# Attention probabilities: transposed on TensorE, or in two of six query tiles by a DRAM round trip and VectorE's 32x32 blocks

## The chip, the cores and the metric

One core of one Trainium2 chip runs the whole kernel as one program. The metric is the device time of one execution in microseconds. The kernel before takes 623.03 us (median of three runs, 622.12 to 624.79).

## The reference

Hash-masked attention over 4 batches of 8 heads, 768 positions and 64 channels, and behind it a gated block on the joined heads:

```python
mask = q_bucket[:, :, :, None] == k_bucket[:, :, None, :]
scores = np.where(mask, scale * np.matmul(q, k.transpose(0, 1, 3, 2)), -1000000000.0)
attn = np.exp(scores - np.max(scores, axis=-1, keepdims=True))
attn = attn / (np.sum(attn, axis=-1, keepdims=True) + 1e-09)
x = np.matmul(attn, v)                      # heads joined to 512 channels
gate = 1.0 / (1.0 + np.exp(-gate_pre))      # gate_pre: causal convolution of x, 5 taps
out = gate * (x @ w_val) @ w_out
```

A bucket is 6 sign bits of a projection. All of it is float32.

## The kernel before

There are 32 **heads** `u` (batch by head) and 6 query **tiles** of 128 rows in each; the main loop runs over the 192 tiles, and **step** `k` is one pass of it. Tile `k` is tile `t = k % 6` of head `k // 6`. Its stages are spread over several steps:

- Scores (line 266, TensorE) are issued one step ahead, in step `k - 1`: 128 x 768 of them, into one of two PSUM buffers `s`. The buffer comes free when the exponentials of tile `k - 2` have read it.
- In step `k` VectorE takes the row maximum `nm` (line 272) and makes factor and shift (`gs` line 278, `nb` line 282); ScalarE computes the exponentials into `p` (line 290), which has four buffers.
- In step `k + 2` GpSimd normalises `p` (line 305).
- In step `k + 3` TensorE transposes `p` in six 128 x 128 blocks (line 314) into two PSUM tiles `tp`, at the end of the step; at the start of step `k + 4` ScalarE copies them to `pt` (line 323), ahead of the exponentials of that step.
- When the sixth tile of a head is copied, `attn_v` (line 337) begins: two of its six rounds of four matmuls `av` in each odd step. ScalarE copies the result to `x` (line 345).

Beside this run side jobs, a few instructions in each step: the preparation of the head after next (`prep`: casts on GpSimd at lines 170 and 173, then six DMAs between partitions at lines 174 to 182, the next raw load at line 148, and for every second head a load of values `vt`, line 154), the convolution (`pair_x`, VectorE, line 368, with a rounding cast `xh` at line 357) and the matrix products of the gated block (`moe`, TensorE, lines 399 and 424, with a rounding cast `hh` at line 408). In some heads' steps the block has no work; in most it issues four matmuls a step.

The orders on TensorE, VectorE, ScalarE and GpSimd are the order of the code. SyncE's queue of DMAs is set by the scheduler that builds the program, and each DMA's wait stands in that queue: what is behind it waits too.

Of the kernel before, what the change touches and what calls it, by code (L numbers as in the profile page):

```python
# [26 lines left out]
def kernel(  # L27
# [13 lines left out]
    D = 64  # L41
# [2 lines left out]
    NP = H // 2  # L44
    KW = 5
    LAG = 3
    scale = 1.0 / float(D) ** 0.5
    NB = 6
    M = D + 2 * NB
# [4 lines left out]
    vp = ctx.enter_context(tc.tile_pool(name="vp", bufs=2))  # L54
    pp = ctx.enter_context(tc.tile_pool(name="pp", bufs=LAG + 1))
    small = ctx.enter_context(tc.tile_pool(name="small", bufs=6))
    ptp = ctx.enter_context(tc.tile_pool(name="ptp", bufs=6))
    xp = ctx.enter_context(tc.tile_pool(name="xp", bufs=2))
    xs = ctx.enter_context(tc.tile_pool(name="xs", bufs=10))
    gp = ctx.enter_context(tc.tile_pool(name="gp", bufs=5))  # L60
# [83 lines left out]
    def load_raw(i):  # L144
        if i < len(units):
            b, h = units[i]
            raws[i] = raw.tile([P, S], FP32, name="r")
            nc.sync.dma_start(out=raws[i], in_=qk[b, h])

    def load_values(i):  # L150
        b, h = units[i]
# [132 lines left out]
    def exponentials(k):  # L284
        s, nb = ss.pop(k), nbs.pop(k)
        p = pp.tile([P, 2, HS], FP32, name="p")
        if k % 2 == 0:
            cur["sm"] = small.tile([P, 2, 2], FP32, name="sm")
        sm = cur["sm"]
        nc.scalar.activation(out=p, in_=s[:, :, 0:HS], func=AF.Exp, bias=nb, scale=gs.pop(k), accum_out=sm[:, k % 2, 0:1])  # L290
        ps[k] = (p.rearrange("p a b -> p (a b)"), sm)


# [9 lines left out]
    def normalise(k):  # L303
        p, _ = ps[k]
        nc.gpsimd.tensor_scalar(out=p, in0=p, scalar1=rcs.pop(k), scalar2=1.0, op0=ALU.mult, op1=ALU.mult)  # L305

    def transposes(k):
        p, _ = ps.pop(k)
        tps[k] = []
        for a in range(2):  # L310
            tp = ps_t.tile([P, 512], FP32, name="tp")
            for n in range(3):
                kb = 3 * a + n
                nc.tensor.transpose(out=tp[:, n * P:(n + 1) * P], in_=p[:, kb * P:(kb + 1) * P], identity=ident)  # L314
            tps[k].append(tp)

    def keep_transposed(k):
        i, qt = tiles[k]
        if qt % 3 == 0:
            cur["pts"].append([ptp.tile([P, 3, HS], FP32, name="pt") for _ in range(2)])  # L320
        qo = (qt % 3) * P
        for pt, tp in zip(cur["pts"][-1], tps.pop(k)):
            nc.scalar.copy(out=pt[:, :, qo:qo + P], in_=tp[:, 0:HS].rearrange("p (a b) -> p a b", b=P))  # L323
        if qt == KB - 1:
            avs.append(attn_v(i, cur["pts"]))
            cur["pts"] = []

    def attn_v(i, pts):
        b, h = units[i]
        hh, c = h % 2, h // 2  # L330
        av = ps_v.tile([P, 512], FP32, name="av")
        vt = vts[i]
        for kb in range(KB):
            if kb:
                yield
            for s, pt in enumerate(pts):
                nc.tensor.matmul(out=av[s * D:(s + 1) * D, 0:HS], lhsT=vt[:, kb, hh * D:(hh + 1) * D], rhs=pt[kb // 3][:, kb % 3, :],  # L337
                                 start=(kb == 0), stop=(kb == KB - 1), tile_position=(0, s * D))
        if hh == 0:
            x = cur["x"] = xp.tile([P, S + KW - 1], FP32, name="x")  # L340
            nc.gpsimd.memset(x[:, 0:KW - 1], 0.0)
        x = cur["x"]
        for s in range(2):
            o = KW - 1 + s * HS
            nc.scalar.copy(out=x[hh * D:(hh + 1) * D, o:o + HS], in_=av[s * D:(s + 1) * D, 0:HS])  # L345
        if hh == 1:
            if c == 0:
                cur["xs"], cur["g"] = {}, []
            convs.append(pair_x(b, c, x, cur["g"], cur["xs"]))

    def pair_x(b, c, x, gs, xs_):
        for o in (0, HS):
            xh = xs.tile([P, HS], FP32R, name="xh")
            xl = xs.tile([P, HS], FP32R, name="xl")
            xs_[(c, o)] = (xh, xl)
            x0 = x[:, KW - 1 + o:KW - 1 + o + HS]
            nc.vector.tensor_copy(out=xh, in_=x0)  # L357
            nc.gpsimd.tensor_tensor(out=xl, in0=x0, in1=xh.bitcast(FP32), op=ALU.subtract)  # L358
        yield
        g = gp.tile([P, S], FP32, name="g")  # L360
        gs.append(g)
        for k in range(KW):
            yield
            w = cw_sb[:, c * KW + k:c * KW + k + 1]
            if k == 0:
                nc.gpsimd.tensor_scalar(out=g, in0=x[:, 0:S], scalar1=w, scalar2=1.0, op0=ALU.mult, op1=ALU.mult)  # L366
            else:
                nc.vector.scalar_tensor_tensor(out=g, in0=x[:, k:k + S], scalar=w, in1=g, op0=ALU.mult, op1=ALU.add)  # L368
        if c == NP - 1:
            yield  # L370
            for g in gs:
                nc.scalar.activation(out=g, in_=g, func=AF.Sigmoid)
            cur["gates"] = 2
            moes.append(moe(b, xs_, gs))
# [9 lines left out]
    def moe(b, xs_, g):  # L384
        hs = {}
        todo = []

        def later():
            while todo:
                todo.pop(0)()  # L390

        def val(o, j):
            acc = acc_tile()
            m = 0
            for wi, xi in ((0, 0), (1, 0), (0, 1)):
                if m:
                    yield
                for c in range(NP):
                    nc.tensor.matmul(out=acc[:, 0:HS], lhsT=wv[wi][:, c, j * P:(j + 1) * P],  # L399
                                     rhs=xs_[(c, o)][xi], start=(m == 0), stop=(m == 11))  # L400
                    m += 1
                later()
            ht = hp.tile([P, HS], FP32, name="ht", bufs=2)
            nc.vector.tensor_tensor(out=ht, in0=acc[:, 0:HS], in1=g[j][:, o:o + HS], op=ALU.mult)  # L404

            def split():
                hh = hp.tile([P, HS], FP32R, name="hh")
                nc.vector.tensor_copy(out=hh, in_=ht)  # L408
                hl = hp.tile([P, HS], FP32R, name="hl")
                nc.gpsimd.tensor_tensor(out=hl, in0=ht, in1=hh.bitcast(FP32), op=ALU.subtract)  # L410
                hs[(o, j)] = (hh, hl)
            todo.append(split)
            yield

        def outp(o, tb):
            for gens in weights:
                finish(gens)
            acc = acc_tile()
            m = 0
            for hi, wi in ((0, 0), (0, 1), (1, 0)):  # L420
                if m:
                    yield
                for j in range(NP):
                    nc.tensor.matmul(out=acc, lhsT=hs[(o, j)][hi][:, tb * P:(tb + 1) * P],  # L424
                                     rhs=wo[wi][:, j, :], start=(m == 0), stop=(m == 11))
                    m += 1
                later()
            ob = op.tile([P, 512], FP32, name="o")
            if cur["gates"]:
                nc.vector.tensor_copy(out=ob, in_=acc)  # L430
            else:
                nc.scalar.copy(out=ob, in_=acc)
            r0 = o + tb * P
            nc.sync.dma_start(out=out[b, r0:r0 + P, :], in_=ob)
            yield

        def idle(n):
            for _ in range(n):
                later()
                yield  # L440

        def hold():
            while len(moes) < 2 and not cur["end"]:
                yield

        chunks = [(val, 0, j) for j in range(NP)]
        chunks += [(val, HS, 0)] + [(outp, 0, tb) for tb in range(3)] + [(val, HS, j) for j in range(1, NP)]
        chunks += [(idle, 2)] + [(outp, HS, tb) for tb in range(3)]
        if b < B - 1:
            chunks.insert(-2, (hold,))  # L450
        for f, *args in chunks:
            yield from f(*args)
# [3 lines left out]
    tiles = [(i, qt) for i in range(len(units)) for qt in range(KB)]  # L456

    raws, stacks, vts, ss, nbs, ps, tps, sums, rcs, nms, gs, cur = {}, {}, {}, {}, {}, {}, {}, {}, {}, {}, {}, {}
    avs, convs, moes, early = [], [], [], {}
    accs = [(ps_m, "m")]  # L460

# [9 lines left out]
        while gens:  # L471
            step(gens)

    cur["gates"], cur["end"], cur["pts"] = 0, False, []
    N = len(tiles)
    with tc.manual_schedule(engines=ENGINES):
        for i in range(5):
# [10 lines left out]
        ahead = [early_bits()]  # L488
        turn = 0
        for k in range(N + LAG + 1):  # L490
            if 0 <= k - LAG - 1:
                keep_transposed(k - LAG - 1)
            pair = k % 2 == 0 and 0 <= k - 2 < N
            if k < N:
# [6 lines left out]
                recip(k - 2)  # L501
            if 0 <= k - 2 < N:
                normalise(k - 2)
            if k < N:
                shifts(k)
            if k + 1 < N:
# [3 lines left out]
                scores(k + 1)  # L510
            if k < N:
                exponentials(k)
            if k >= 60 or k % 2:
                step(convs)
            for _ in range((1, 0, 2, 0, 2, 2)[k % 6]):
# [10 lines left out]
            if k % 2:  # L526
                step(avs)
                step(avs)
            if 0 <= k - LAG < N:
                transposes(k - LAG)  # L530
        accs[:] = [(ps_m, "m"), (ps_t, "tp"), (ps_s, "s"), (ps_t, "tp"), (ps_s, "s")]
        finish(avs)
# [65 lines left out]
```

## Time and profile before

| | us |
|---|---|
| median of three runs | 623.03 |
| span of the profiled execution, first to last instruction | 620.8 |
| busy in it: TensorE matmul / VectorE / ScalarE / GpSimd | 585.5 / 437.6 / 421.4 / 395.6 |
| the steps that the change touches, by ScalarE's exponentials | 175.4 to 545 |
| mean busy share of the 16 DMA engines in those steps | 0.34 |

The profile gives the profiled execution no time but its span; the 2.2 us between the span and the median of the runs lie around the program. Span times count from the first instruction. In a row of groups stand the line, the engine, the operation, what it writes and reads, the count, then the busy time, the mean of one in ns, and the engine's idle time ahead with what ended it. PE is TensorE, DVE VectorE, ACT ScalarE, POOL GpSimd, SPq the queue of SyncE.

### The profile page before, as it was taken

The numbers are of one execution on the slowest core, as the hardware profiler recorded it, in microseconds if no ns is written. First come the engines' busy times: TensorE is split into PE (matmuls) and PEld (weight loads), VectorE is DVE, ScalarE is ACT, GpSimd is POOL, SyncE is SP. The second block draws the span as 40 slices with busy tenths as digits, with TensorE's granted clock in tenths as the row PEclk, the third lists the DMA queues.
The fourth block names the chain that finished last, engine by engine and source line by source line (L and its number), as shares of the span: only waits on it lengthen the run. The fifth ranks groups of instructions, "written<-read, shape, count | busy, mean of one in ns | idle before, by whom it ended". The sixth has DMA issues, their size and how long they took to land.

```text
span 620.8 us, 10648 instructions
## 1 busy us (share of the span) xinstructions
PE 585.5 (94%) x3496; PEld 423.4 (68%) x3496; DVE 437.6 (70%) x1017; ACT 421.4 (68%) x881; POOL 395.6 (64%) x373
## 2 busy tenths in 40 slices
PE   5789898989999999999999999999999999999997
PEld 2655565555657777776767777777667877775895
DVE  5869798998975866668575867569665877665532
ACT  2777777778778666777787676777787766765400
POOL 3576868778766765578564777568764777544321
PEclk9799999999999999999999999999999999999999
DMA  6467666564532235243433234333422213200111
GB/s 227 123 197 199 200 167 208 157 175 118 133 83 68 70 79 142 72 108 82 122 82 107 61 80 126 84 115 82 108 70 78 67 42 91 69 18 1 51 52 51
DMA packets 29031, 64.64 MB, mean 104 GB/s; under 512 B 4937, under 2 KB 10057, under 8 KB 28977
## 3 DMA queue, kind: packets, MB, share of 16 engines
q1 hardware_dynamic: 28832, 63.93, 37.8%
q8 instruction: 28, 0.46, 0.3%
q14 instruction: 27, 0.21, 0.1%
q10 hardware_dynamic: 144, 0.03, 0.0%
HBM read 30.60 MB, written 7.86 MB: 62 GB/s over the span
## 4 chain that ended last, share of the span: by engine, by line
PE 66%; DVE 12%; ACT 12%; DMA 5%; issue 3%; POOL 2%; SPq 1%; ACTq 0%; POOLq 0%; DVEq 0%
PE av L337 17%; PE s L266 16%; PE tp L314 12%; PE m L424 8%; PE m L399 7%; ACT p L290 5%; DVE nm L272 4%; ACT pt L323 3%; ACT x L345 2%; DMA w<-in_w_val_dram 2%; DVE g L368 2%; PE tp L399 1%; PE tp L424 1%; PE s L424 1%; DMA bk<-bq 1%
## 5 line engine op out<-in xcount | busy, mean ns | idle before, releaser
L305 POOL TENSOR_SCALAR p<-p,ri 128x768 f32<-128x768 f32 x192 | 210.5, 1100 | 156.0 <-DVE nb L282 130.8
L272 DVE TENSOR_REDUCE nm<-s 128x1 f32<-128x768 f32 x192 | 182.5, 950 | 61.2 <-PE s L266 61.0
L290 ACT ACTIVATE p<-s,nb,gs 128x768 f32<-128x768 f32 x192 | 192.6, 1003 | 46.2 <-DVE nb L282 41.9
L323 ACT COPY pt<-tp 128x384 f32<-128x384 f32 x384 | 165.7, 485 | 75.3 <-PE tp L314 74.4
L314 PEld LDWEIGHTS tp<-ident,p 128*128 128x128 f32 x1152 | 130.3, 142 | 72.2 <-issue 43.6
L314 PE MATMUL tp<-ident,p 128*128 128x128 f32 x1152 | 164.4, 279 | 2.6 <-ACT pt L323 2.1
L337 PE MATMUL av<-pt,vt 128*64 128x384 f32 x768 | 144.9, 498 | 0.0
L266 PE MATMUL s<-ak,aq 76*128 76x384 f32 x384 | 118.1, 389 | 23.2 <-ACT p L290 19.7
L266 PE MATMUL s<-bk,bq 128*128 128x384 f32 x384 | 101.3, 345 | 0.4 <-DVE bq L252 0.4
L337 PEld LDWEIGHTS av<-pt,vt 128*64 128x64 f32 x768 | 47.0, 136 | 61.5 <-issue 61.4
L266 PEld LDWEIGHTS s<-ak,aq 76*128 76x128 f32 x384 | 59.2, 194 | 38.7 <-ACT p L290 34.6
L368 DVE SCALAR_TENSOR_TENSOR g<-x,cw_sb,g 128x768 f32<-128x768 f32 x64 | 79.4, 1241 | 2.2 <-POOL g L366 2.1
L266 PEld LDWEIGHTS s<-bk,bq 128*128 128x128 f32 x384 | 71.7, 194 | 0.8 <-issue 0.8
L173 POOL TENSOR_TENSOR bq<-r,aq 128x768 fp32r<-128x768 f32 x31 | 59.2, 1909 | 0.1
L410 POOL TENSOR_TENSOR hl<-ht,hh 128x384 fp32r<-128x384 f32 x32 | 32.3, 1009 | 39.5 <-DVE hh L408 39.5
L345 ACT COPY x<-av 64x384 f32<-64x384 f32 x64 | 30.4, 475 | 29.7 <-PE av L337 29.0
L282 DVE TENSOR_SCALAR nb<-nm,gs 128x1 f32<-128x1 f32 x192 | 40.4, 211 | 3.5
L399 PE MATMUL m<-xh,wv 128*128 128x384 f32 x200 | 42.7, 337 | 0.0
L358 POOL TENSOR_TENSOR xl<-x,xh 128x384 fp32r<-128x384 f32 x32 | 33.4, 1059 | 13.8 <-DVE xh L357 13.8
L290 ACT ACTIVATION_READ_ACCUMULATOR p<-s,nb,gs 128x1 f32 x192 | 39.0, 203 | 0.0
L404 DVE TENSOR_TENSOR ht<-m,g 128x384 f32<-128x384 f32 x25 | 13.9, 556 | 35.6 <-PE m L399 29.2
L424 PE MATMUL m<-wo,hh 128*128 128x512 f32 x144 | 38.1, 394 | 0.0
(86 smaller groups left out, 486.9 us busy)
## 6 DMA issues: line engine op xcount, KB each, us to landing
r<-in_qk_dram SPq DMA_DIRECT2D x32, 384.0 KB
vt<-in_v_dram SPq DMA_DIRECT2D x16, 384.0 KB
out_dram<-o SPq DMA_DIRECT2D x24, 256.0 KB
ak<-aq SPq DMA_DIRECT2D x31, 192.0 KB
bk<-aq SPq DMA_DIRECT2D x31, 192.0 KB
bk<-bq SPq DMA_DIRECT2D x31, 192.0 KB
bq<-aq SPq DMA_DIRECT2D x31, 192.0 KB
hh<-in_qk_dram SPq DMA_DIRECT2D x16, 192.0 KB
```

The costliest lines, as they stand in the source:

```text
L173: nc.gpsimd.tensor_tensor(out=bq, in0=r, in1=aq.bitcast(FP32), op=ALU.subtract)
L266: nc.tensor.matmul(out=s[:, hf, 0:HS], lhsT=lq[0:n, qs], rhs=rk[0:n, hf * HS:(hf + 1) * HS], start=n == M, stop=n == P)
L272: nc.vector.tensor_reduce(out=nm, in_=s[:, :, 0:HS], axis=AX.XY, op=ALU.max, negate=True)
L290: nc.scalar.activation(out=p, in_=s[:, :, 0:HS], func=AF.Exp, bias=nb, scale=gs.pop(k), accum_out=sm[:, k % 2, 0:1])
L305: nc.gpsimd.tensor_scalar(out=p, in0=p, scalar1=rcs.pop(k), scalar2=1.0, op0=ALU.mult, op1=ALU.mult)
L314: nc.tensor.transpose(out=tp[:, n * P:(n + 1) * P], in_=p[:, kb * P:(kb + 1) * P], identity=ident)
L323: nc.scalar.copy(out=pt[:, :, qo:qo + P], in_=tp[:, 0:HS].rearrange("p (a b) -> p a b", b=P))
L337: nc.tensor.matmul(out=av[s * D:(s + 1) * D, 0:HS], lhsT=vt[:, kb, hh * D:(hh + 1) * D], rhs=pt[kb // 3][:, kb % 3, :], start=(kb == 0), s ...
L345: nc.scalar.copy(out=x[hh * D:(hh + 1) * D, o:o + HS], in_=av[s * D:(s + 1) * D, 0:HS])
L368: nc.vector.scalar_tensor_tensor(out=g, in0=x[:, k:k + S], scalar=w, in1=g, op0=ALU.mult, op1=ALU.add)
L399: nc.tensor.matmul(out=acc[:, 0:HS], lhsT=wv[wi][:, c, j * P:(j + 1) * P], rhs=xs_[(c, o)][xi], start=(m == 0), stop=(m == 11))
L424: nc.tensor.matmul(out=acc, lhsT=hs[(o, j)][hi][:, tb * P:(tb + 1) * P], rhs=wo[wi][:, j, :], start=(m == 0), stop=(m == 11))
```

## The change

For tiles 0 and 2 of heads 10 to 30 (steps 60 to 185: 42 tiles of 192) the transposes of line 314 and the copies of line 323 go. Instead:

- the exponentials write `p` in an order of columns in which the 32 columns that belong to one partition group lie together (`g a j x`);
- `put_out`, in step `k + 2` behind the normalisation, writes `p` (384 KB) to DRAM with one DMA;
- `take_in`, in step `k + 3`, reads it back with four DMAs of 32 partitions x 4 x 192 elements, one for each partition group, into `pt`;
- `turn_blocks`, in step `k + 6` behind `nb`, turns each 32 x 32 block in place on VectorE with one instruction over 128 x 768.

`pt` becomes one tile of 128 x 3 x 4 x 6 x 32 instead of two, in three buffers instead of six (the same bytes), so that `av` reads it in runs of 32 columns for all heads, and the copies of the other tiles write it so. The casts `xh` and `hh` go from VectorE to ScalarE in steps 60 to 191 (45 casts).

```diff
-    ptp = ctx.enter_context(tc.tile_pool(name="ptp", bufs=6))
+    ptp = ctx.enter_context(tc.tile_pool(name="ptp", bufs=3))
+    def by_blocks(k):
+        return FIRST <= k < LAST and k % KB in (0, 2)
...
-        nc.scalar.activation(out=p, in_=s[:, :, 0:HS], func=AF.Exp, bias=nb, scale=gs.pop(k), accum_out=sm[:, k % 2, 0:1])
+        to, of = p, s[:, :, 0:HS]
+        if by_blocks(k):
+            to = p.rearrange("p a b -> p (a b)").rearrange("p (g a j x) -> p a j g x", g=G, a=2, x=QB)
+            of = of.rearrange("p a (j g x) -> p a j g x", g=G, x=QB)
+        nc.scalar.activation(out=to, in_=of, func=AF.Exp, bias=nb, scale=gs.pop(k), accum_out=sm[:, k % 2, 0:1])
...
+    def put_out(k):
+        p, _ = ps.pop(k)
+        pds[k] = dram.tile([P, S], FP32, name="pd")
+        nc.sync.dma_start(out=pds[k], in_=p)
+    def take_in(k):
+        w = place(k)
+        rows = pds.pop(k).rearrange("(i q) (g c) -> g q i c", q=QB, g=G)
+        for g in range(G):
+            nc.sync.dma_start(out=w[g * QB:(g + 1) * QB].rearrange("q i j x -> q i (j x)"), in_=rows[g])
+    def turn_blocks(k):
+        w = place(k).rearrange("p i j x -> p (i j x)")
+        nc.vector.transpose(out=w, in_=w)
+        placed(k)
...
-                nc.tensor.matmul(out=av[s * D:(s + 1) * D, 0:HS], lhsT=vt[:, kb, hh * D:(hh + 1) * D], rhs=pt[kb // 3][:, kb % 3, :],
+                nc.tensor.matmul(out=av[s * D:(s + 1) * D, 0:HS], lhsT=vt[:, kb, hh * D:(hh + 1) * D], rhs=pt[:, :, :, kb, :],
...
+    def rounded(out, in_):
+        if FIRST <= cur["k"] < N:
+            nc.scalar.copy(out=out, in_=in_)
+        else:
+            nc.vector.tensor_copy(out=out, in_=in_)
...
+                if by_blocks(k - 2):
+                    put_out(k - 2)
...
+            if by_blocks(k - 6):
+                turn_blocks(k - 6)
...
+            if by_blocks(k - LAG):
+                take_in(k - LAG)
+            elif 0 <= k - LAG < N:
                 transposes(k - LAG)
```

Lines move with it: what stood at 148, 154, 174 to 177, 181 and 182 stands at 151, 161, 181 to 184, 188 and 189, scores at 273, maxima at 279, `av` at 376, transposes at 358. Below are rows of the built programs' order (line, operation, what it writes and reads, its size), with the semaphores that a DMA waits for: a DMAHW semaphore is that of an earlier DMA, the others are engines.

**TensorE**, from the scores of tile 88 in step 87 to those of tile 91 in step 90, before:

```order
L266 MATMUL s<-ak,aq 128x384 x2
L266 MATMUL s<-bk,bq 128x384 x2
L399 MATMUL m<-xl,wv_120 128x384 x4
L337 MATMUL av<-pt,vt 64x384 x4
L314 MATMUL tp<-ident,p 128x128 x6
L266 MATMUL s<-ak,aq 128x384 x2
L266 MATMUL s<-bk,bq 128x384 x2
L399 MATMUL m<-xh,wv_120 128x384 x4
L314 MATMUL tp<-ident,p 128x128 x6
```

and now:

```order
L273 MATMUL s<-ak,aq 128x384 x2
L273 MATMUL s<-bk,bq 128x384 x2
L444 MATMUL m<-xl,wv_120 128x384 x4
L376 MATMUL av<-pt,vt 64x384 x4
L273 MATMUL s<-ak,aq 128x384 x2
L273 MATMUL s<-bk,bq 128x384 x2
L444 MATMUL m<-xh,wv_120 128x384 x4
L358 MATMUL tp<-ident,p 128x128 x6
```

The six transposes between `av` and the next scores are gone; it is the same two steps later (tile 86). Tiles 0 and 2 are transposed in odd steps, so that it is always the odd step, the one with `av`, that loses them.

**SyncE's queue** for head 14 (steps 84 to 91). Before, from the first DMA of a preparation to the load of values:

```order
L182 DMA ak_3551<-ud_428 12x768 [waits DMAHW4_49,PE_49]
L174 DMA ak_3551<-aq_3550 64x768 [waits Pool_49]
L175 DMA bk_3553<-aq_3550 64x768 [waits PE_49]
L176 DMA bk_3553<-bq_3552 64x768 [waits Pool_49]
L181 DMA aq_3550<-ud_428 12x768 [waits DMAHW6_49,DMAHW5_49,DMAHW0_49]
L148 DMA r_3601<-in_qk_dram 128x768 [waits DMAHW1_49]
L177 DMA bq_3552<-aq_3550 64x768 [waits DMAHW7_49,DMAHW2_49]
L154 DMA vt_3548<-in_v_dram 128x768 [waits DMAHW3_49,PE_49]
```

and now (`pd_3377` is tile 84, `pd_3444` tile 86):

```order
L322 DMA pd_3377<-p_3298 128x768 [waits DMAHW4_49,Pool_49]
L322 DMA pd_3444<-p_3386 128x768 [waits Pool_49]
L189 DMA ak_3496<-ud_426 12x768 [waits PE_49]
L329 DMA pt_3430<-pd_3377 32x4x192 [waits DMAHW4_49,DVE_49]
L329 DMA pt_3430<-pd_3377 32x4x192 [waits DMAHW0_49]
L329 DMA pt_3430<-pd_3377 32x4x192 [waits DMAHW1_49]
L329 DMA pt_3430<-pd_3377 32x4x192 [waits DMAHW2_49]
L161 DMA vt_3493<-in_v_dram 128x768 [waits DMAHW3_49,PE_49]
L329 DMA pt_3430<-pd_3444 32x4x192 [waits DMAHW5_49]
L329 DMA pt_3430<-pd_3444 32x4x192
L329 DMA pt_3430<-pd_3444 32x4x192 [waits DMAHW6_49]
L329 DMA pt_3430<-pd_3444 32x4x192 [waits DMAHW7_49]
```

The reads of tile 84 stand behind the write of tile 86 (which waits for GpSimd's normalisation in step 88), and those of tile 86 behind the load of values, whose wait for TensorE is for the last `av` of the head before, in step 91. The preparation's copies come after all of them.

**VectorE** in steps 90 to 92, before:

```order
L282 TENSOR_SCALAR nb<-nm,gs 128x1
L404 TENSOR_TENSOR ht<-m,g 128x384
L272 TENSOR_REDUCE nm<-s 128x1
L278 TENSOR_SCALAR gs<-nm 128x1
L282 TENSOR_SCALAR nb<-nm,gs 128x1
L272 TENSOR_REDUCE nm<-s 128x1
```

and now:

```order
L289 TENSOR_SCALAR nb<-nm,gs 128x1
L334 STREAM_TRANSPOSE pt<-pt 128x768
L449 TENSOR_TENSOR ht<-m,g 128x384
L279 TENSOR_REDUCE nm<-s 128x1
L285 TENSOR_SCALAR gs<-nm 128x1
L289 TENSOR_SCALAR nb<-nm,gs 128x1
L279 TENSOR_REDUCE nm<-s 128x1
```

The turn of tile 84 stands behind the shift of step 90 and ahead of the row maximum of step 91; it waits for the four reads. Here as everywhere it is in an even step.

More of the change, by code (lines that the diff above doesn't have):

```diff
@@ L46 @@
     LAG = 3
+    QB = 32
+    G = P // QB
+    FIRST, LAST = 60, B * H * KB - KB
     scale = 1.0 / float(D) ** 0.5
@@ L305, in normalise, with place, placed @@
         nc.gpsimd.tensor_scalar(out=p, in0=p, scalar1=rcs.pop(k), scalar2=1.0, op0=ALU.mult, op1=ALU.mult)
+    def put_out(k):
[11 more added lines that the diff above has]
+        placed(k)
+    def place(k):
+        i, qt = tiles[k]
+        at = pts.setdefault(i, {})
+        if qt // 3 not in at:
+            at[qt // 3] = ptp.tile([P, 3, G, KB, QB], FP32, name="pt")
+        return at[qt // 3][:, qt % 3]
+    def placed(k):
+        i, _ = tiles[k]
+        done[i] = done.get(i, 0) + 1
+        if done[i] == KB:
+            avs.append(attn_v(i, pts.pop(i)))
     def transposes(k):
@@ L317, in keep_transposed @@
     def keep_transposed(k):
[L318 to L326, printed above, removed]
+        for a, tp in enumerate(tps.pop(k)):
+            nc.scalar.copy(out=place(k)[:, :, 3 * a:3 * a + 3].rearrange("p i j x -> p j i x"),
+                           in_=tp[:, 0:HS].rearrange("p (j i x) -> p j i x", i=G, x=QB))
+        placed(k)
     def attn_v(i, pts):
@@ L335, in attn_v @@
                 yield
-            for s, pt in enumerate(pts):
-                nc.tensor.matmul(out=av[s * D:(s + 1) * D, 0:HS], lhsT=vt[:, kb, hh * D:(hh + 1) * D], rhs=pt[kb // 3][:, kb % 3, :],
+            for s, pt in sorted(pts.items()):
+                nc.tensor.matmul(out=av[s * D:(s + 1) * D, 0:HS], lhsT=vt[:, kb, hh * D:(hh + 1) * D], rhs=pt[:, :, :, kb, :],
                                  start=(kb == 0), stop=(kb == KB - 1), tile_position=(0, s * D))
@@ L356, in pair_x @@
             x0 = x[:, KW - 1 + o:KW - 1 + o + HS]
-            nc.vector.tensor_copy(out=xh, in_=x0)
+            rounded(out=xh, in_=x0)
             nc.gpsimd.tensor_tensor(out=xl, in0=x0, in1=xh.bitcast(FP32), op=ALU.subtract)
@@ L407, in split @@
                 hh = hp.tile([P, HS], FP32R, name="hh")
-                nc.vector.tensor_copy(out=hh, in_=ht)
+                rounded(out=hh, in_=ht)
                 hl = hp.tile([P, HS], FP32R, name="hl")
@@ L458 @@
     raws, stacks, vts, ss, nbs, ps, tps, sums, rcs, nms, gs, cur = {}, {}, {}, {}, {}, {}, {}, {}, {}, {}, {}, {}
+    pds, pts, done = {}, {}, {}
     avs, convs, moes, early = [], [], [], {}
@@ L472, in finish @@
             step(gens)
-    cur["gates"], cur["end"], cur["pts"] = 0, False, []
+    cur["gates"], cur["end"] = 0, False
     N = len(tiles)
@@ L490 @@
         for k in range(N + LAG + 1):
-            if 0 <= k - LAG - 1:
+            cur["k"] = k
+            if 0 <= k - LAG - 1 and not by_blocks(k - LAG - 1):
                 keep_transposed(k - LAG - 1)
@@ L528 @@
                 step(avs)
-            if 0 <= k - LAG < N:
+            if by_blocks(k - LAG):
+                take_in(k - LAG)
+            elif 0 <= k - LAG < N:
                 transposes(k - LAG)
```

## The prediction

> **What bounds the kernel now.** First the page's head and the busy times over the touched steps (columns: window, length, then busy time of PE, PEld, DVE, ACT, POOL, granted clock, DMA share, GB/s).
>
> ```profile
> span 620.8 us, 10648 instructions
> PE 585.5 (94%) x3496; PEld 423.4 (68%) x3496; DVE 437.6 (70%) x1017; ACT 421.4 (68%) x881; POOL 395.6 (64%) x373
> ...
> 175.40:545.00 369.60, 364.16 (x2202) 270.59 (x2202) 256.20 (x612) 274.05 (x574) 244.56 (x229) 1.00 0.34 88
> ```
>
> TensorE is busy for 364.2 of 369.6 us there, at full clock; no other engine is above 274. Then the groups of that window, to see what the transposes are and who waits.
>
> ```profile
> L323 ACT COPY pt<-tp 128x384 f32<-128x384 f32 x251 | 108.4, 485 | 57.7 <-PE tp L314 57.2
> L314 PE MATMUL tp<-ident,p 128*128 128x128 f32 x750 | 105.9, 277 | 0.7 <-ACT pt L323 0.3
> L266 PE MATMUL s<-ak,aq 76*128 76x384 f32 x250 | 75.0, 381 | 4.7 <-ACT p L290 4.1
> L408 DVE CAST hh<-ht 128x384 fp32r<-128x384 f32 x21 | 12.9, 612 | 0.0
> L357 DVE CAST xh<-x 128x384 fp32r<-128x384 f32 x20 | 12.6, 633 | 5.8 <-ACT x L345 4.3
> ```
>
> ScalarE waits for TensorE (57 us); TensorE waits for exponentials only 4.1 us. Last the chain of waits in two pairs of steps of head 20 (start, length, piece):
>
> ```profile
> 371.33 0.65 PE tp L314 x6
> 371.99 0.70 PE s L266 x4
> 372.69 0.70 PE m L399 x4
> 373.39 1.44 PE av L337 x8
> 374.83 0.81 PE tp L314 x6
> 375.64 0.71 PE s L266 x4
> 376.35 0.93 PE m L424 x4
> 377.28 0.66 PE tp L314 x6
> 377.94 0.81 PE s L266 x4
> 378.74 0.93 PE m L424 x4
> 379.68 1.44 PE av L337 x8
> 381.12 0.80 PE tp L314 x6
> 381.92 0.18 PE s L266
> ```
>
> Where the gated block works, the chain is TensorE alone. So what leaves TensorE shortens those steps, until something else is late.
>
> **What the change takes away.** A tile's six transposes are a piece of 0.65 to 0.81 us in that chain, mean 0.73. 42 tiles x 0.73 = **30.7 us**. (The group's 105.9 us over 125 tiles would be 0.85 each; it counts pipelined neighbours twice, so I take the chain.) ScalarE loses 84 copies of 0.485 us, 40.7 us, and gets 45 casts; its nearest row is that same copy of 128x384, so 21.8 us. VectorE loses those casts, 45 x 0.62 = 28 us. Neither bounds the window, so I cost both at nothing; TensorE's work is the cover, and without it ScalarE's balance would be the difference, 19 us to the good.
>
> The exponentials' new column order, the copies into runs of 32 and `av` reading runs of 32 have no row. The largest of them on the path is `av`, by the page's chain (shares of the span by line):
>
> ```profile
> PE av L337 17%; PE s L266 16%; PE tp L314 12%; PE m L424 8%; PE m L399 7%; ACT p L290 5%; DVE nm L272 4%; ACT pt L323 3%; ACT x L345 2%; DMA w<-in_w_val_dram 2%; DVE g L368 2%; PE tp L399 1%; PE tp L424 1%; PE s L424 1%; DMA bk<-bq 1%
> ```
>
> 17% of 620.8 is 105 us in all 192 tiles; a tenth more would be 11 us. I take nothing, since no column is read or written twice, and keep 0 to +11.
>
> **What it adds: the way through DRAM.** Its price is time, not bandwidth: 42 x 0.79 MB are 33 MB over 370 us, 89 GB/s beside today's 88. What matters is when the last of four reads lands, because VectorE's turn waits for it, and behind the turn, in VectorE's order, stands the next row maximum. The prices, head 14's rows:
>
> ```profile
> 268.28 0.46 SPq L176 DMA_DIRECT2D bk<-bq  x1
> 268.85 0.49 SPq L181 DMA_DIRECT2D aq<-ud  x1
> 269.38 0.37 SPq L148 DMA_DIRECT2D r<-in_qk_dram  x1
> 269.74 1.51 PE L337 MATMUL av<-pt,vt 128*64 128x384 f32 x8
> 270.93 0.47 SPq L177 DMA_DIRECT2D bq<-aq  x1
> ...
> 274.40 0.94 DVE L272 TENSOR_REDUCE nm<-s 128x1 f32<-128x768 f32 x1
> 275.38 0.15 DVE L278 TENSOR_SCALAR gs<-nm 128x1 f32<-128x1 f32 x1
> 275.56 0.22 DVE L282 TENSOR_SCALAR nb<-nm,gs 128x1 f32<-128x1 f32 x1
> 275.88 0.99 ACT L290 ACTIVATE p<-s,nb,gs 128x768 f32<-128x768 f32 x1 [0.74 <-DVE nb L282]
> 276.77 0.19 ACT L290 ACTIVATION_READ_ACCUMULATOR p<-s,nb,gs 128x1 f32 x1
> ```
>
> An issue takes SyncE 0.37 to 0.49 us: 0.5 for each read. L177 waits for L176 to land: issued by 268.74, landed at 270.93, 2.2 us. That copy stays in SBUF. The other end is the program's first load from DRAM, beside five larger ones:
>
> ```profile
> 0.73 0.41 ACTq L74 DMA_DIRECT2D packed<-in_proj_dram  x1
> 4.54 0.19 DVE L77 TENSOR_TENSOR proj_sb<-packed 128x32 f32<-128x32 f32 x1 [4.54 <-DMA packed<-in_proj_dram]
> ```
>
> Issued by 1.14, used at 4.54: 3.4 us. I take **2.5 us** for a read, nearer to the row in the loop, as the queue there is the one that these reads meet; 2.2 to 3.4 stays in the range. [...] The turn is one VectorE pass over 128x768; the row maximum, a pass of the same length, takes 0.94, so 0.95. (Ends: the `hh` cast at its mean, two of 0.61, 1.2; half a pass, 0.5.) From the turn's end to free scores: maximum to shift 1.4 (274.40 to 275.78), exponentials 1.1 with a gap of 0.1 (275.78 to 276.96). So **from a late read's issue order on**: reads x 0.5 + 2.5 + 0.95 + 1.4 + 1.2, then the scores two tiles later can start.
>
> Three places, by the built queue:
>
> *Reads of tile 2 behind a value load* (even heads 12 to 28, nine of them). The load waits for the `av` of step 6u+7; 0.4 us for it, then n reads: 6.45 + 0.5 n from `av`'s end to the scores of tile 6u+11. What TensorE has to do meanwhile: head 20, 374.83 to 381.92 is 7.09, less the 0.80 that goes, 6.3. Head 14, with less of the block's work:
>
> ```profile
> 276.78 0.87 PE L314 MATMUL tp<-ident,p 128*128 128x128 f32 x6
> 277.41 0.60 PE L266 MATMUL s<-ak,aq 76*128 76x384 f32 x2
> ```
>
> 271.25 to 277.4, 6.2, less 0.73: 5.4. Heads 12, 18, 20, 26, 28 have n = 1 and are like head 20: 6.95 - 6.3 = 0.65 each, 3.3 us. Heads 14, 22, 16, 24 have n = 4, 3, 2, 2 and are like head 14: 3.05, 2.55, 2.05, 2.05, together 9.7 us. Sum 13.
>
> *Reads of tile 0 behind a preparation's first copy* (heads 15, 16, 25), which waits for the cast in step 6u+5:
>
> ```profile
> 280.30 1.54 POOL L170 CAST aq<-r 128x768 fp32r<-128x768 f32 x1
> ...
> 287.44 0.59 PE L266 MATMUL s<-ak,aq 76*128 76x384 f32 x2
> ```
>
> The cast ends at 281.84; 0.5 for the copy and 4 x 0.5 + 6.05 make 8.55, and the scores of tile 99 would come 5.6 - 0.7 = 4.9 later: 3.6 late in head 15. In 16 the value load has taken the loss already; 25 lies between, some 2. Sum 5.6.
>
> *Reads of tile 0 behind the write of tile 2* (most others): 0.5 + 4 x 0.5 + 6.05 = 8.55 from the normalisation in step 6u+4.
>
> ```profile
> 261.01 1.02 POOL L305 TENSOR_SCALAR p<-p,ri 128x768 f32<-128x768 f32 x1 [4.33 <-PE tp L314]
> ...
> 271.81 0.60 PE L266 MATMUL s<-ak,aq 76*128 76x384 f32 x2
> ```
>
> Head 14: 262.03 to 271.8, less 0.73, 9.0: just hidden. I take 1 us for two shorter heads.
>
> Smaller: without the transposes between `av` and the next scores, an exponential that ended under them is waited for where the block issues nothing, about eight odd steps; one such wait stands at 0.3 us, so 2 to 3. The 42 turns (40 us) replace 28 us of casts on VectorE: 256 - 28 + 40 = 268 of some 360 us, no bound. The Trainium skill, "Vector Engine (DVE) Microarchitecture Reference", where it describes the reshape block, has the 32x32 turn at one element per cycle and lane: an estimate of 0.8 us with the 0.96 GHz it gives; no trace here shows it, and by it the late places would come 2 us nearer.
>
> **Sum:** -30.7 + 13 + 5.6 + 1 + 2.5 = -8.6; span 620.8 - 8.6 = 612.2. The median of the runs lies 2.2 above the span: **614.4 us**.
>
> **Rivals.**
>
> *All hidden.* For it: TensorE's order has slack that a chain of averages misses, and ScalarE, freed of 19 us, starts exponentials sooner. Against: the value load's wait is fixed in the queue. -30.7 gives 592.3; with a third of the losses left, 600.
>
> *Slower: reads land late.* Each further microsecond delays nine heads by 9, three by 3, and of the twelve just hidden about 5: 17 us per us of landing. The sum passes zero at 2.5 + 8.6 / 17 = 3.0 us. For it: 3.4 us at the start, a doubled load on the queues, and the value load (384 KB) directly ahead. Against: 2.2 with a raw load of 384 KB behind. At 3.7 us: 614.4 + 20.4 = 634.8.
>
> *No gain: the round of maximum, exponential and scores takes over.* Where the block issues little (heads 15, 16, 23 and 24 have it in every second step only) waits of 0.3 us for exponentials are there already, and a transpose that goes may only lengthen them. If half of the 30.7 us is cover of this kind, 614.4 + 15 = 629; with a quarter, 622, no change.
>
> **Chances.** Forecast 0.42 (604 to 619); hidden 0.2 (590 to 604); landing 0.24 (626 to 645); taken over 0.14 (617 to 629). A measurement of this kernel tells 0.5%, 3 us, from no change. Faster by more: 0.58 (the forecast but for its end, and hidden); within: 0.16 (most of taken over, the ends of two others); slower: 0.26. The range of 8 in 10, from most of the hidden case to half of the late one, is 595 to 635; the forecast's own, 604 to 619.
>
> **What would show it.** In the profile after: 252 fewer transposes and 42 turns of about 0.95 us; VectorE's waits put down to the reads, 3 to 5 us long in step 6u+8 of the even heads and in step 6u+6 of heads 15 and 25, near nothing elsewhere; TensorE idle behind exponentials for some 20 us more than now; reads landing 2.5 us after their issue; `av` as long as before. If VectorE's waits come in every head, the landing is what I had wrong; if there are few waits and the time is still near 623, the gain was cover.

## The result, and the profile after

The changed kernel takes 695.89 us (median of four runs, 694.92 to 696.16) beside 623.3 us of the kernel before on the same chip: ratio 1.1166, 95% interval 1.1141 to 1.1191. It is 73 us slower; the prediction was 614.4 us. Of the runs below, three had one execution each in a slower state (3145.66 us of `before_av3`, 1873.52 of `pp5`, 643.67 of `blocks_av3_act_pool`), which their medians here leave out.

First the page of the changed kernel: its head, and the groups (columns as before: busy time, mean ns, then idle time ahead and what ended it).

```profile
span 694.4 us, 10607 instructions
...
PE 585.2 (84%) x3244; PEld 403.9 (58%) x3244; DVE 450.1 (65%) x1014; ACT 404.1 (58%) x842; POOL 383.6 (55%) x373
...
L363 ACT COPY pt<-tp 128x384 f32<-128x384 f32 x300 | 129.6, 486 | 118.7 <-PE av L376 100.0
L273 PE MATMUL s<-ak,aq 76*128 76x384 f32 x384 | 122.1, 399 | 74.9 <-ACT p L301 72.5
L376 PE MATMUL av<-pt,vt 128*64 128x384 f32 x768 | 147.5, 504 | 1.5 <-DVE pt L334 1.4
L334 DVE STREAM_TRANSPOSE pt<-pt 128x768 f32<-128x768 f32 x42 | 41.1, 978 | 48.8 <-DMA pt<-pd 48.8
```

The 252 transposes are gone (1152 to 900) and there are 42 turns of 0.98 us. But the copies to `pt`, which waited only for their own transposes before, now wait 100 us for **`av`**, and TensorE's scores wait 72.5 us for exponentials. In the kernel before, those two engines waited so (engine, line, what is waited for; us in total, times, longest):

```profile
ACT pt L323 <- PE tp L314: 74.4, 95, 2.1
...
PE s L266 <- ACT p L290: 19.7, 32, 1.8
```

The windows show where the time went: first the touched steps (60 to 185), then all before them (columns as in the prediction: window, length, busy time of PE, PEld, DVE, ACT, POOL, granted clock, DMA share, GB/s).

```profile
185.70:617.10 431.40, 361.86 (x1958) 252.37 (x1958) 271.25 (x611) 256.64 (x533) 232.31 (x229) 0.98 0.53 151
0.00:185.70 185.70, 153.32 (x918) 96.17 (x919) 145.11 (x339) 123.69 (x263) 125.08 (x119) 0.98 0.56 160
```

The touched steps take 431.4 us instead of 369.6, and TensorE stands idle for 69.5 of them instead of 5.4. Step 60 starts at 185.7 instead of 175.4: ten microseconds are lost before the first tile goes through DRAM. So something slows heads in which nothing but the layout of `pt` has changed. The waits of the changed kernel (columns as above; PEld is TensorE's loading of weights ahead of a matmul):

```profile
PEld s L273 <- ACT p L301: 111.3, 124, 2.9
ACT pt L363 <- PE av L376: 100.0, 31, 5.0
...
DVE pt L334 <- DMA pt<-pd: 48.8, 22, 5.2
...
ACT p L301 <- PE tp L358: 40.2, 13, 4.2
```

Three waits are new; the kernel before has none of them. I call them **W** (copies for `av`: 31 times in 32 heads), **P** (exponentials for transposes, 13 times) and **D** (turns for reads, 22 times).

W in the timeline of the changed kernel, around step 121 (start, length, engine, line; in brackets the idle time before and what ended it):

```profile
397.98 1.51 PE L376 MATMUL av<-pt,vt 128*64 128x384 f32 x8
...
399.52 0.86 ACT L363 COPY pt<-tp 128x384 f32<-128x384 f32 x2 [4.57 <-PE av L376]
...
400.27 1.01 ACT L301 ACTIVATE p<-s,nb,gs 128x768 f32<-128x768 f32 x1
...
401.42 0.62 PE L273 MATMUL s<-ak,aq 76*128 76x384 f32 x2 [0.43 <-ACT p L301]
```

The copies of tile 3 of head 19 stand at the start of step 121 in ScalarE's order, the exponentials behind them. They need a `pt` buffer. The three whole tiles are held by head 18 (two) and by tiles 0 to 2 of head 19; head 18's come free only with its last `av`, which stands at the *end* of step 121 on TensorE. Before, `pt` was cut by key blocks: the two half tiles with blocks 0 to 2 were read for the last time by the third of six `av` rounds, in step 6u+5, and by the built order the two copies took just those. "The same bytes" as three tiles instead of six are not the same number of moments at which something comes free.

### The profile page after: what moved, and what is told of

Its sections match the earlier page's. It is cut to its first block, busy times and chain, and to the rows that moved or that the text cites. A ratio compares the mean times of both kernels' runs of the same rounds, so it can differ in the third digit from the quotient of the medians.

```text
span 694.4 us, 10607 instructions
## 1 busy us (share of the span) xinstructions
PE 585.2 (84%) x3244; PEld 403.9 (58%) x3244; DVE 450.1 (65%) x1014; ACT 404.1 (58%) x842; POOL 383.6 (55%) x373
## 5 line engine op out<-in xcount | busy, mean ns | idle before, releaser
L316 POOL TENSOR_SCALAR p<-p,ri 128x768 f32<-128x768 f32 x192 | 197.1, 1031 | 201.8 <-DVE nb L289 119.8
L363 ACT COPY pt<-tp 128x384 f32<-128x384 f32 x300 | 129.6, 486 | 118.7 <-PE av L376 100.0
L273 PE MATMUL s<-ak,aq 76*128 76x384 f32 x384 | 122.1, 399 | 74.9 <-ACT p L301 72.5
L358 PE MATMUL tp<-ident,p 128*128 128x128 f32 x900 | 129.0, 281 | 23.7 <-ACT pt L363 21.7
L376 PE MATMUL av<-pt,vt 128*64 128x384 f32 x768 | 147.5, 504 | 1.5 <-DVE pt L334 1.4
L358 PEld LDWEIGHTS tp<-ident,p 128*128 128x128 f32 x900 | 103.5, 143 | 72.0 <-issue 33.9
L413 DVE SCALAR_TENSOR_TENSOR g<-x,cw_sb,g 128x768 f32<-128x768 f32 x64 | 77.7, 1213 | 3.8 <-POOL g L411 3.5
L334 DVE STREAM_TRANSPOSE pt<-pt 128x768 f32<-128x768 f32 x42 | 41.1, 978 | 48.8 <-DMA pt<-pd 48.8
L307 DVE TENSOR_SCALAR s<-sm 128x2 f32<-128x2 f32 x96 | 18.2, 190 | 53.8 <-ACT p L301 53.7
L469 PE MATMUL m<-wo,hh 128*128 128x512 f32 x144 | 39.8, 408 | 0.0
```

What stands on the lines that cost most here:

```text
L273: nc.tensor.matmul(out=s[:, hf, 0:HS], lhsT=lq[0:n, qs], rhs=rk[0:n, hf * HS:(hf + 1) * HS], start=n == M, stop=n == P)
L334: nc.vector.transpose(out=w, in_=w)
L363: nc.scalar.copy(out=place(k)[:, :, 3 * a:3 * a + 3].rearrange("p i j x -> p j i x"), in_=tp[:, 0:HS].rearrange("p (j i x) -> p j i x", i= ...
```

## The experiments

All ratios are to the kernel before on the same chip.

**1. The layout alone, and `av` earlier.** `layout3` is the changed kernel with no tile through DRAM and the casts on VectorE; `av3` puts three `av` rounds each into steps 6u+3 and 6u+5, so that `pt` is free before step 6u+7.

```diff
# layout3, from the changed kernel
-        return FIRST <= k < LAST and k % KB in (0, 2)
+        return False
-        if FIRST <= cur["k"] < N:          # rounded
+        if False:
# *_av3, from layout3, the kernel before and the changed kernel
-            if k % 2:
+            if k % 6 in (3, 5):
+                step(avs)
```

Expected of `layout3`, `before_av3` (the control), `layout_av3` and `blocks_av3`, in this order:

> The changed kernel without its DRAM trip: no tile goes by blocks, casts stay on VectorE; only the new shape of pt (one tile for all six key blocks, three buffers) is left. Theory W (the copy of tile 3 of a head, at the start of step 6u+7, now waits for the last av of the head before, issued at the end of that step, since a whole tile is freed only then): 31 such waits on ScalarE of 2 to 5 us as in the changed kernel, and 655 to 700 us. Theory D (reads from DRAM land late and VectorE's turns wait): no waits of copies for av, 620 to 626 us.

> The kernel before with three rounds of av in steps 6u+3 and 6u+5 each, instead of two in each of three odd steps: a control for the next two. Both theories: within 1% of 623 us.

> As layout3, with av done by step 6u+5 as in the control, so that the whole tile is free before the copy of step 6u+7 wants it. W: no copy waits for av, and the time is the control's within 1%. If av reading runs of 32 columns were dear, it would be 5 to 15 us above the control, with longer av rows. D: the control's time.

> The changed kernel whole, with av done by step 6u+5. W alone: the waits for av are gone and the time falls from 696 to what the recorded sum gave, about 614, at most 625. D: it stays above 680. If both hold, between: the waits for av gone, the turns' waits for reads (48.8 us in the changed kernel) still there, 630 to 660.

Measured: `layout3` 674.49 (ratio 1.0826, 1.0787 to 1.0864); `before_av3` 633.24 (1.0163, 1.0136 to 1.0191); `layout_av3` 633.1 (1.0158, 1.0137 to 1.0179); `blocks_av3` 678.75 (1.0886, 1.0864 to 1.0908). The control missed its expectation: `av` in two steps instead of three costs some 10 us by itself. The layout without one block through DRAM is already 8% slower, and with `av` early it equals its control. So W is real. But with W gone the DRAM trip, with the casts on ScalarE that go with it, still costs 46 us (678.75 against 633.1). That is nearest to theory D, yet the turns of `blocks_av3` wait only 19.9 us for reads, beside 48.8 in the changed kernel. In its waits the copies no longer wait for `av`; P has stayed:

```profile
PEld s L273 <- ACT p L301: 88.5, 90, 5.1
...
PE s L273 <- ACT p L301: 63.5, 64, 4.8
...
ACT p L301 <- PE tp L358: 43.7, 11, 5.6
```

P in the timeline of `blocks_av3`, in step 130 (tile 4 of head 21):

```profile
414.44 2.16 PE L376 MATMUL av<-pt,vt 128*64 128x384 f32 x12
...
416.53 0.61 PE L273 MATMUL s<-ak,aq 76*128 76x384 f32 x2
...
418.26 0.82 PE L358 MATMUL tp<-ident,p 128*128 128x128 f32 x6
418.45 0.32 SPq L322 DMA_DIRECT2D pd<-p  x1
...
419.16 0.99 ACT L301 ACTIVATE p<-s,nb,gs 128x768 f32<-128x768 f32 x1 [4.72 <-PE tp L358]
...
420.29 0.62 PE L273 MATMUL s<-ak,aq 76*128 76x384 f32 x2 [1.22 <-ACT p L301]
```

The exponentials of tile 4 need one of four buffers `p`. Tile 0's should be free, since its only reader now is its write to DRAM. But SyncE's queue has that write so late that by the built order, in 14 of the 21 touched heads of the changed kernel (16 in `blocks_av3`), the exponentials take the buffer of tile 1 instead, whose transposes stand at the end of the *same* step on TensorE. ScalarE waits 4.7 us for TensorE, and TensorE then for ScalarE.

**2. The write from another queue, `av` spread otherwise, a fifth buffer.** `_act` issues the write from ScalarE's queue behind the exponentials of step k+2; `2121` spreads `av` as 2, 1, 2, 1 rounds over steps 6u+3 to 6u+6; `pp5` leaves the changed kernel as it is but for a fifth `p` buffer (and one staging buffer less for the output, to make room).

```diff
# *_act
-        nc.sync.dma_start(out=pds[k], in_=p)
+        nc.scalar.dma_start(out=pds[k], in_=p)
...
             if k < N:
                 exponentials(k)
+            if by_blocks(k - 2):
+                put_out(k - 2)
# *_2121
-            if k % 2:
-                step(avs)
+            for _ in range((1, 0, 0, 2, 1, 2)[k % 6]):
                 step(avs)
# pp5
-    pp = ctx.enter_context(tc.tile_pool(name="pp", bufs=LAG + 1))
+    pp = ctx.enter_context(tc.tile_pool(name="pp", bufs=LAG + 2))
-    op = ctx.enter_context(tc.tile_pool(name="op", bufs=2))
+    op = ctx.enter_context(tc.tile_pool(name="op", bufs=1))
```

Expected of `blocks_av3_act`, `layout_2121`, `blocks_2121`, `blocks_2121_act` and `pp5`:

> As blocks_av3, with the write to DRAM issued from ScalarE's queue, behind the exponentials of step k + 2, so that the exponentials of tile 6u+4 take the buffer of tile 6u (written out long ago) and not that of tile 6u+1, which is transposed only at the end of the same step. Theory P (this wait on the p buffer is what blocks_av3 has lost: 43.7 us of waits of ScalarE for transposes, the odd gap of 4.7 to 5.8 us ahead of the fifth exponential of a head against 4.1 in layout_av3): 635 to 650 us, the waits of exponentials for transposes gone. Theory D (late reads, 19.9 us of waits of VectorE's turns): no more than a few us gained, 670 to 680.

> As layout3 (no blocks, casts on VectorE, three whole buffers), with the six rounds of av in steps 6u+3 to 6u+6 as 2, 1, 2, 1: done before the copy of step 6u+7. A control for the next two. Theory W: no copy waits for av; 620 to 634 us, where an even spread costs less than three rounds at once.

> The changed kernel with that spread of av, and nothing else: the p buffer as in the changed kernel. P: the fifth exponential of most heads still waits for transposes, 650 to 670 us. If W were all: the control less up to 20 us.

> The same with the write issued from ScalarE's queue: neither wait for av nor for the p buffer is left, only the reads. W and P together: the control or less, 605 to 630 us; what is left of waits of turns for reads (three places of the prediction) costs up to 20 us of the 30 that the transposes free. D: 650 or more.

> The changed kernel with five p buffers instead of four (room for it from the output staging tile, one buffer instead of two), and nothing else: the wait of the fifth exponential for the transposes of the second tile goes, the wait of copies for av stays. Theory P: between layout3's 674 and the changed kernel's 696, about 675 to 685. If that wait costs nothing beside the other one: 693 to 699.

Measured: `blocks_av3_act` 634.4 (1.0186, 1.0162 to 1.021), 44 us under `blocks_av3`; `layout_2121` 637.53 (1.0231), no better than `av3`; `blocks_2121` 670.68 (1.0766) and `blocks_2121_act` 636.02 (1.021), 35 us apart; `pp5` 680.89 (1.0944, 1.0909 to 1.0979), by the ratios 14 us under the changed kernel. `layout_2121`, `blocks_2121` and `blocks_2121_act` all came out above their ranges. In the waits of `blocks_av3_act` P has left the list, and the scores' wait is halved:

```profile
PE s L273 <- ACT p L301: 32.2, 48, 1.6
```

The edit does a second thing, though: SyncE's queue loses the write that stood ahead of the reads, and D falls too, from 19.9 us to 2.2 (from 37.0 to 17.2 in the `2121` pair). So the 35 to 44 us are those of P and of earlier reads together. `pp5` leaves the queue as it is and has no wait of kind P, while D rises from 48.8 to 62.1 us: the 14 us are P's, beside W. No run takes P alone away where W is out; that W covered part of P would fit these numbers and is not shown by itself.

And yet `blocks_av3_act` only equals its control `layout_av3` (1.0186 and 1.0158). With both waits out, the trip gains nothing.

**3. Half tiles.** `half_layout` keeps the new column order, but in six half tiles by key blocks as before, with no tile through DRAM; `half` has the DRAM trip with it (eight reads of half size a tile and two turning instructions); `half_act` adds the write from ScalarE's queue; `half_act_dve` puts the casts back on VectorE.

```diff
-    ptp = ctx.enter_context(tc.tile_pool(name="ptp", bufs=3))
+    ptp = ctx.enter_context(tc.tile_pool(name="ptp", bufs=6))
-            at[qt // 3] = ptp.tile([P, 3, G, KB, QB], FP32, name="pt")
+            at[qt // 3] = [ptp.tile([P, 3, G, 3, QB], FP32, name="pt") for _ in range(2)]
...
-                ... rhs=pt[:, :, :, kb, :],
+                ... rhs=pt[kb // 3][:, :, :, kb % 3, :],
```

> The new order of columns in pt, but in half tiles again (three key blocks each, six buffers, as before the change), no blocks, casts on VectorE, av in the odd steps as before the change. Theory W: no copy waits for av and av reads runs of 32 at no cost: 620 to 626 us, the kernel before. If the layout itself were dear, above 630.

> The changed kernel with pt in half tiles and nothing else (a tile is read back by eight DMAs of half the size, and turned by two instructions). It takes the wait for av away and leaves the wait on the p buffer (fifth exponential of a head behind the transposes of its second tile). P: 655 to 675 us. If that wait weighed nothing here: 605 to 630.

> As half, with the write to DRAM issued from ScalarE's queue, so that the p buffer of tile 0 is free for tile 4. W and P together explain the loss: 605 to 630 us, the waits of exponentials for transposes gone. What is left above 593 is late reads and casts.

> As half_act, with the casts xh and hh on VectorE as before the change. If ScalarE's casts hold up GpSimd (its subtractions wait for them, and the normalisations behind it in order), this is 5 to 15 us faster than half_act. If VectorE has no room for them beside the turns, it is slower by 5 to 10. Equal: the casts are no matter.

Measured: `half_layout` 622.09 (0.9994, 0.998 to 1.0009); `half` 713.95 (1.1466); `half_act` 671.05 (1.0785); `half_act_dve` 679.65 (1.0926). The first is the cleanest result: column order, copies and `av` in runs of 32 cost nothing, so all of `layout3`'s loss, 674.5 - 622.1 = **52.4 us**, is W. The copies' longest wait by total in `layout3`, and in `half_layout`, where none for `av` is left:

```profile
ACT pt L363 <- PE av L376: 92.0, 31, 3.8
```

```profile
ACT pt L366 <- PE tp L361: 74.0, 95, 2.1
```

With half tiles and the trip I missed by far (see the expectations). Eight reads take SyncE's queue twice as long as four. In `half_act` the turns wait 84 us for them, and TensorE's `av` for the turns:

```profile
DVE pt L337 <- DMA pt<-pd: 84.1, 28, 6.1
...
PEld av L379 <- DVE pt L337: 23.5, 10, 3.4
```

That the issues are what costs the 49 us by which `half_act` stands above `half_layout` fits these waits, but was not tested: the rows that a read moves are half as long as well (384 bytes for 768), and no run parts the two. `half` minus `half_act` is 43 us, the size of the step from `blocks_av3` to `blocks_av3_act`; here too P goes (33.3 us to 2.9) and D falls with it (103.8 to 84.1). The casts did not explain the rest: back on VectorE they made it 8.6 us slower there.

**4. What leaving the transposes out can gain, and what the casts cost.** `drop` is `half_layout` without the transposes and copies of the 42 tiles, and without the trip: GpSimd clears their columns of `pt` instead of normalising, so the attention of those rows is left out of the result. `half_layout_casts` is `half_layout` with the casts on ScalarE from step 60. `blocks_av3_act_pool` and `blocks_av3_act_dve` are `blocks_av3_act` with the casts on GpSimd and on VectorE; `blocks_356_act_dve` is the last with `av` in rounds of two in steps 6u+3, 6u+5 and 6u+6.

```diff
# drop, from half_layout
+    def fill(k):
+        ps.pop(k)
+        rcs.pop(k)
+        for t in place(k):
+            nc.gpsimd.memset(t, 0.0)
...
+                if by_blocks(k - 2):
+                    fill(k - 2)
+                else:
+                    normalise(k - 2)
# blocks_356_act_dve, from blocks_av3_act_dve
-            if k % 6 in (3, 5):
-                step(avs)
-                step(avs)
+            for _ in range((2, 0, 0, 2, 0, 2)[k % 6]):
                 step(avs)
```

> half_layout (the kernel before in the new column order) with the transposes and copies of tiles 0 and 2 of heads 10 to 30 left out and nothing in their place: GpSimd clears their columns of pt instead of normalising p, so the output is not the reference's. What is left is the ceiling of the change. Theory G (the removed transposes bound TensorE, as the prediction's 30.7 us had it): 590 to 600 us. Theory H (they were mostly cover for the wait for exponentials): 608 to 622.

> half_layout with the casts on ScalarE from step 60 on, as in the change: this part of the change alone. No matter: 620 to 625 us. If ScalarE, which is behind TensorE and ahead of the exponentials, is held up by them: 625 to 640.

> As blocks_av3_act, with the casts xh and hh on GpSimd, which subtracts right behind them, instead of ScalarE. In blocks_av3_act GpSimd waits 17.3 and 9.2 us for ScalarE's casts, and TensorE's transposes 13.2 us for late normalisations behind them. If that is where the gain went: 615 to 625 us. If not: 630 to 638, or more, as GpSimd gets 21 us of work.

> This is blocks_av3_act (634.4) with the casts xh and hh back on VectorE; its control without the trip is layout_av3 (633.1). If the casts on ScalarE are what eats the trip's gain there (they cost 5.2 in half_layout_casts), it comes to about 629, 4 to 6 under blocks_av3_act. If the late reads and the turns on VectorE eat it (rival), VectorE now has casts and turns both, and it stays at 634 or goes over it, as half_act_dve was 8.6 over half_act.

> The same as blocks_av3_act_dve, but with av in rounds of two in steps 6u+3, 6u+5 and 6u+6 (three rounds in each of two steps cost 11 us in the control before_av3): still one step ahead of the copies of the next head's tile 3. If the 11 us come from three rounds standing in one step, this gives back up to 8 of them: 621 to 629, as fast as the kernel before or a little under it. If any shift of av away from the odd steps costs that much (as layout_2121 at 637.5 says), 630 to 640.

Measured: `drop` 603.25 (0.9698, 0.9674 to 0.9722); `half_layout_casts` 627.27 (1.0077, 1.0058 to 1.0096); `blocks_av3_act_pool` 635.32 (1.0211, 1.0178 to 1.0243); `blocks_av3_act_dve` 624.9 (1.0041, 1.0018 to 1.0063); `blocks_356_act_dve` 627.69 (1.0097, 1.0073 to 1.0121).

`drop` sets the ceiling: 622.1 - 603.25 = **18.8 us**, not 30.7; the time lies between those of the two theories. It is a generous ceiling, since `drop` also spares GpSimd the normalising of those tiles (244.2 us busy in the touched steps, 231.0 in `drop`) and leaves their `p` without a reader. The touched steps, in `half_layout` and in `drop`:

```profile
176.80:546.40 369.60, 364.17 (x2202) 270.57 (x2202) 256.08 (x612) 274.05 (x574) 244.18 (x229) 1.00 0.34 88
```

```profile
175.80:526.00 350.20, 340.38 (x1956) 245.55 (x1956) 260.98 (x612) 242.57 (x492) 230.96 (x271) 1.00 0.36 93
```

TensorE's busy time falls by 23.8 us, and its idle time rises from 5.4 to 9.8: of 30.7 us by the chain's pieces a fifth never was a gain, and 4.4 us more go to idle time. The scores' wait for exponentials, 20.7 us in `half_layout`, is 26.2 in `drop`.

The casts on ScalarE cost 5 us by themselves; on GpSimd they gain nothing (1.0211 beside 1.0186). Moved back to VectorE they save some 9 us in `blocks_av3_act_dve` (1.0186 to 1.0041), more than I expected, and there the trip does gain: 1.0041 against the control's 1.0158, some 7 us. The touched steps, in `layout_av3` and in `blocks_av3_act_dve`:

```profile
183.20:557.00 373.80, 363.09 (x2204) 274.38 (x2206) 262.03 (x611) 272.71 (x572) 235.97 (x227) 1.00 0.33 86
```

```profile
184.30:551.50 367.20, 344.66 (x1958) 255.88 (x1960) 295.13 (x650) 242.54 (x490) 229.93 (x227) 0.98 0.62 177
```

TensorE does 18.4 us less and the steps shorten by 6.6; the other 11.8 are idle time, and what TensorE waits for is exponentials (the scores' wait in these steps: 18.5 us, beside 6.3 in `layout_av3`). Reads are no longer late there (four waits, 2.6 us in all). VectorE works 33 us more, since turns and casts both stand on it ahead of the maxima; that these 33 us are what delays the exponentials fits the windows and was not tested by itself. The other spread of `av` (`blocks_356_act_dve`) did not give back the 10 us that `before_av3` costs over the kernel before. No version here beats the kernel before: the best with the trip, `blocks_av3_act_dve`, is 0.4% slower.

## Why the prediction was wrong

**The step that failed** is the one that costed the edits without a row: "I take nothing, since no column is read or written twice, and keep 0 to +11." That sentence asked what `av` and the copies cost while they run, and there it was right (`half_layout`; in the touched steps an `av` matmul takes 503 ns in the changed kernel, 499 in `half_layout` and before). It did not ask when a buffer of `pt` comes free. Three whole tiles for six halves put the release two steps later, behind work that waits for the waiting engine: 52.4 us by themselves.

**The second failure** is in the list of added waits. I followed the four reads through SyncE's queue but took the write only as something ahead of reads. Whoever reads `p` last sets when the exponentials three or four tiles on may write, and the last reader of tile 0 had become a queue whose order a scheduler sets. What is late next should have been asked for `p` too: 14 us beside W; without W some 40, together with the reads that the same edit moves forward.

The other terms:

- *-30.7 for 42 tiles.* The transposes went, but the ceiling is -18.8. The rival "no gain: the round takes over" named this cover and priced half of the gain; the measured loss is 39%, and of its 11.9 us only 4.4 are idle time.
- *Casts on ScalarE at nothing.* 5.2 us by themselves. I had put 19 us of relief for ScalarE; the rows show GpSimd, which subtracts behind each cast and normalises behind that, waiting longer for casts: 54.6 us in `half_layout`, 67.0 in `half_layout_casts`. How 5 us of the time come from it was not followed further. First the waits of `half_layout`, then those of `half_layout_casts`:

```profile
POOL hl L458 <- DVE hh L397: 39.4, 16, 9.3
...
POOL xl L406 <- DVE xh L397: 15.2, 13, 5.7
```

```profile
POOL hl L458 <- DVE hh L397: 23.3, 8, 9.3
POOL xl L406 <- ACT xh L395: 23.0, 11, 3.4
...
POOL xl L406 <- DVE xh L397: 10.4, 6, 5.6
POOL hl L458 <- ACT hh L395: 10.3, 7, 3.0
```

- *Late reads, +13 for tile 2 and +5.6 for tile 0.* The places of tile 2 were exactly right: in the changed kernel the turns wait in heads 12, 14, 16 and so on to 28, nine times, 20.7 us in sum, if 1.6 to 3.4 us each and not the 3 to 5 of the prediction. For tile 0 I named heads 15, 16 and 25 and had the others just hidden; 13 heads wait there, 28 us in sum. Two of each, of the changed kernel, with the reads of the third (tile 2 of head 14) on SyncE's queue ahead of it:

```profile
248.15 0.98 DVE L334 STREAM_TRANSPOSE pt<-pt 128x768 f32<-128x768 f32 x1 [1.30 <-DMA pt<-pd]
257.16 0.98 DVE L334 STREAM_TRANSPOSE pt<-pt 128x768 f32<-128x768 f32 x1 [1.68 <-DMA pt<-pd]
...
292.39 0.36 SPq L161 DMA_DIRECT2D vt<-in_v_dram  x1
292.81 1.84 SPq L329 DMA_DIRECT2D pt<-pd  x4
...
297.91 0.98 DVE L334 STREAM_TRANSPOSE pt<-pt 128x768 f32<-128x768 f32 x1 [3.19 <-DMA pt<-pd]
310.99 0.98 DVE L334 STREAM_TRANSPOSE pt<-pt 128x768 f32<-128x768 f32 x1 [3.65 <-DMA pt<-pd]
```

- *2.5 us for a read.* Too short for tile 2. The four reads above are issued by 294.65, and the turn starts 3.26 us later; over the nine late tiles 2, which all stand behind the load of values, it is 3.1 to 4.9 us, over the 13 late tiles 0 it is 1.9 to 3.9. In the chain of waits of `blocks_av3`, where only tiles 0 are late, the last of four reads begins its issue at 296.63 and lands 2.54 us after, and the turn starts 0.13 us behind that:

```profile
296.15 0.44 SPq L329
296.59 0.04 issue
296.63 2.54 DMA pt<-pd
299.17 0.03 issue
```

  So the rival "late landing" was right in part: the median over the 22 late turns is 3.15 us, 3.0 without the 0.13, and by the prediction's 17 us for each microsecond of landing that is worth some 9 us, an estimate. It is not what made the kernel slower than before: `layout3`, which reads nothing back, is 8% slower already. The turn itself, 0.98 us against 0.95, was right.

The parts come near the measured time: 614.4 + 52.4 (W) + 14 (P beside W) + 11.9 (the ceiling) + 5.2 (casts) = 698, measured 695.9. Each was measured in another kernel, they cover one another, and the late reads beyond the prediction's 19.6 us are not among them, so that the sum comes so close is luck and no evidence. None of the rivals held W or P: my range ended at 635 because every case in it was one of prices and landings, none one of buffers.

## What to carry to other kernels

When an edit regroups a buffer pool, write down for each tile its last reader, the step and place in which that reader stands, and who needs the buffer next; a pool of fewer, larger tiles of the same size in bytes can close a ring between two in-order engines, and it does so in all work that uses the pool, not only in the part that was changed. Do the same for a tile whose reader moves to another engine or to a DMA queue. And price what leaves the bounding engine by an experiment that only leaves it out, since that ceiling (18.8 us here for 30.7 of work) is what all costs are to be set against.

## What the runs showed of the hardware

- The 32x32 turn of 128x768 float32 in place takes 978 ns on VectorE, and one of 128x384 takes 578 ns in `half` (533 to 537 for most of those that directly follow another turn): 400 ns for 384 elements more in a lane, 1.04 ns each, and 0.18 us fixed if the two lie on a line. The Trainium skill's page "Vector Engine (DVE) Microarchitecture Reference", where it describes the reshape block, has one element per cycle and lane, 1.04 ns at its 0.96 GHz; the two sizes agree with it, and what the estimate of 0.8 us lacked is the fixed part.
- Twice as many reads of half the size cost about twice SyncE's time, since each issue takes as long as one of full size. In SyncE's timeline of `half`, eight reads of 48 KB stand there for 3.75 us, 0.47 each, beside 1.84 us, 0.46 each, for the four of 96 KB above:

```profile
333.19 3.75 SPq L330 DMA_DIRECT2D pt<-pd  x8
```

- TensorE's busy time hardly fell with the work: 361.9 us in the changed kernel's touched steps, 364.2 before, while `drop`, with the same transposes gone, has 340.4. Two things in the trace go that way; how much each is worth was not worked out. Of the 250 score matmuls on `ak` in those steps, the 66 that start after a wait of over 0.15 us are counted 449 ns long in the mean, the others 379. And behind some waits the granted clock stands at half for some microseconds: TensorE waits 2.62 us until 315.87, and in the window from 314 to 321 the clock is 0.53. The eight `av` matmuls at its end take 2.05 us, the eight ahead of it 1.51:

```profile
314.00:321.00 7.00, 5.13 (x18) 3.86 (x20) 6.60 (x15) 5.82 (x13) 2.80 (x3) 0.53 0.47 147
...
310.23 1.51 PE L376 MATMUL av<-pt,vt 128*64 128x384 f32 x8
...
320.16 2.05 PE L376 MATMUL av<-pt,vt 128*64 128x384 f32 x8
```

  Over the touched steps the clock is 0.98 instead of 1.00, some 2% of 431 us or 9 us of the time at the most, an estimate. So part of what W, P and D cost may be the slower clock behind the waits; no run parts it from the waits themselves.
